# Two tap products of a short convolution as one VectorE instruction, under a new instruction plan

## The chip, the core and the metric

The kernel runs on one core of one Trainium2 chip. The metric is device time in microseconds, the median of three runs. A profile was taken of one further execution; all engine times below are of that one. PE is TensorE, DVE is VectorE, ACT is ScalarE, POOL is GpSimd, SP is the queue from which nearly all DMAs are issued.

## What is computed

Two independent blocks over 2048 positions and 576 channels, whose outputs stand side by side in the result.

```python
# A: short shift convolution of k (4 taps), gate by v, long convolution, gate by q
k_shift = sum(k_pad[:, t:t + S, :] * shift_k[:, ks - 1 - t] for t in range(4))
kv = k_shift * v
y = irfft(rfft(kv, 2S) * rfft(ssm_k, 2S))[:S] + kv * ssm_D
a = q * y
# B: linear attention, 32 heads of 18 channels
q, k, v = split(x @ wqkv)
pq, pk = phi(q), phi(k)           # phi(t) = t + 1 if t > 0 else exp(t), + 1e-6
kv = einsum("bhsd,bhse->bhde", pk, v);  z = pk.sum(s)
o = einsum("bhqd,bhde->bhqe", pq, kv) / (einsum("bhqd,bhd->bhq", pq, z) + 1e-6)
b = o.reshape(B, S, D) @ wo
out = concat([a, b], -1)
```

## The kernel before

**Recording and issuing.** The body records operations (`P.op`, `load`) with what they read and write. `_issue` then takes two constants: PLAN is a list of words such as `D836`, an engine letter and the number of a recorded operation, and it fixes both the engine of each operation and the order on every engine; PLACES gives each buffer its SBUF offset or PSUM bank. Nothing is decided at run time: each engine runs its list from first to last and waits at each instruction for what it depends on, including the earlier users of the same bytes or banks. For products and sums of two SBUF operands (those recorded with `two=1`) a GpSimd instruction is also made to wait for the VectorE one that stands last before it in PLAN.

**Block A.** The position is split as 16 a + b: a is the partition (128), b runs over 16, loaded in two halves (bh = 0, 1) of eight b each. Channels go in three chunks (cc = 0, 1, 2) of 192. `conv_piece(cc, bh)` makes the gated short convolution of one such half chunk:

```python
for i in (0, 2):
    P.op("D", lambda e, i=i: tap(e, i), rd=[kh, ...], wr=[(m, i)], name="tap", n=3072, ...)
```

`tap(e, i)` is one VectorE product (L402) of k at shifts i and i + 1 with the broadcast weights Wj, into the quarters i and i + 1 of a scratch tile m of 4 x 8 x 192 elements a partition. Then the two halves of m are summed (3072 elements; for the two pieces in ACC by an accumulating DMA that GpSimd issues), then the two quarters (1536), and the sum is multiplied into v (1536). These are all helper line L236. Pieces are called cv and the two digits below (cv00, cv10, ...).

The long convolution is a two-stage transform by matmul. The filter (h) is first transposed on PE (`h_piece`, L437) and copied to hT. Stage one (`s1`, L468) multiplies by the table Gsb in eight groups of four matmuls for each chunk of h and of the gated v (u), each group in two PSUM banks, copied by ACT or DVE (L229, L231) to Ch or Cu. VectorE transposes 32 x 32 blocks (L507), and stage two (`s2`, L516) has for each of nine channel groups and for h and u four groups of four small matmuls. Group kh of a channel group reads the strip of 32 partitions kh (0 to 3) of its tile. DMAs swap rows of the h spectrum into X, VectorE or GpSimd multiplies the spectra (p1, p2 at L236), and `inv` (L552) and `inv2` (L577) transform back; ACT or DVE copies the results to V and yb, and q is multiplied in (q rows of L236).

**Block B.** `kproj` (L624) makes 16 k projections of ten matmuls, each in two PSUM banks: ACT takes an exp (L629), DVE finishes phi (L632) and only then are the banks free. `qproj` (L645, L648, L651) does the same for 20 q pieces of five matmuls and one bank. `b_G` (L674) contracts over the positions, `kvmm` (L709) and `b_M` (L771) fold in the weights; DVE masks the result of L709 (L712, L716); copies of M (ACT or DVE) must all be done before the M sum (`smm`, L799), whose result VectorE writes back (L802). `b_out` (L814) is the output projection, 32 groups of five matmuls.

**Order around the change.** There are eight PSUM banks, and PE, ACT and DVE pass them on. The tap products stand in VectorE's list among the phi steps of the q and k projections (cv00, cv10, cv20) and, for the second half, among the denominators and the G groups (cv01, cv11, cv21).

Of the kernel before, what the change touches and what calls it, by code (L numbers as in the profile page):

```python
# [11 lines left out]
ALU = mybir.AluOpType  # L12

S = 2048
D = 576
# [4 lines left out]
CC = 192  # L20
# [163 lines left out]
def kernel(  # L184
# [13 lines left out]
    nc = tc.nc  # L198
# [13 lines left out]
    P = Prog()  # L212
# [38 lines left out]
    Wj = SB("Wj", [128, 4, D], side=1)  # L251
# [35 lines left out]
    for i in range(2):  # L287
# [8 lines left out]
         rd=[wtok], wr=[(Wj, 0), (Wj, 1)])  # L296
# [94 lines left out]
    def conv_piece(cc, bh):  # L391
        kh, vt = khs[bh], vs[bh]
        c0 = cc * CC
        m = SB("m", [128, 4, 8, CC])

        def tap(e, i):
            base = kh.t[:, i:i + 8, c0:c0 + CC]
            i0 = bass.AP(tensor=base.tensor, offset=base.offset,
                         ap=[list(base.ap[0]), [D, 2], [D, 8], [1, CC]])
            w = Wj.t[:, 2 - i:4 - i, c0:c0 + CC]  # L400
            i1 = bass.AP(tensor=w.tensor, offset=w.offset + D, ap=[list(w.ap[0]), [-D, 2], [0, 8], [1, CC]])
            return nc.vector.tensor_tensor(out=m.t[:, i:i + 2], in0=i0, in1=i1, op=ALU.mult)  # L402
# [469 lines left out]
P98 S423 D35 S19 P95 P368 G0 D37 A15 A99 A369 S18 S41 P366 D100 G228 D367 P101 P375 A96 S472 D97 P372 A102 A377  # L872
A374 D376 P394 G4 D373 S59 D370 A395 P386 P392 D103 G10 G14 P384 P426 D387 A393 P424 G12 S56 G378 D385 A23 D427
P388 A425 P433 D379 G42 A434 P435 P382 S55 G428 D389 D436 P390 P380 P437 D391 A383 P443 D438 A381 P429 D405 P475
P441 A444 P431 D414 S24 S40 S58 P473 A430 A442 D396 P439 A432 A440 S60 P146 P417 A147 P415 S25 A474 G477 D476 D445
A418 P104 D148 A105 P143 S46 P401 P397 A416 P446 P448 S51 D106 P452 A144 P155 A449 A453 A398 D454 A402 P149 P152
A156 A150 D145 A447 S478 P408 D463 G47 D157 A153 P403 P399 P457 D151 A409 D400 S50 S45 P468 P170 A458 A404 P406
D469 P410 P461 D154 A462 D65 P459 P421 P161 A171 A411 P158 S48 A460 P412 S43 P466 P455 G52 D172 P419 D64 A407 A422
P164 D75 A456 P481 D74 D66 P470 A413 A467 P464 S230 P450 A420 P167 A165 G67 A451 A471 A162 D163 P479 A465 A480 A168
P197 D166 P200 A482 P191 A159 A192 D169 A201 D160 A198 D202 D193 P110 P185 D76 A111 G44 G483 D112 D199 P173 S594  # L880
A186 P134 P176 A174 G49 S61 D175 D187 A135 P122 A177 P179 G77 D178 D136 P107 S652 P119 A123 D124 A180 A108 P137 D78
D85 S229 A120 P188 D109 D181 A138 S595 D121 G68 S232 A189 P140 P128 S38 A141 D139 D190 P125 D84 A129 D142 P131 D130
P486 D86 P116 A126 A487 A132 A117 D127 P113 G87 S231 A114 S62 A39 S653 D133 D118 P194 P494 P182 D115 A183 P223 D88
A224 P484 A485 A195 D70 D79 A495 P226 A225 S17 P208 D69 D80 A227 S63 P236 D237 D238 P203 G71 D184 P239 D196 P243
P488 G81 D204 A209 A205 A210 P492 D240 D241 S552 D244 P498 A489 P206 D242 D245 A493 P490 A499 D72 D73 A491 P496
S553 S246 P218 A497 S247 A207 D219 P537 D220 A538 P531 S259 P529 A530 P221 P533 D82 S260 S258 P527 A532 A222 S254
D83 A534 P535 D89 A536 S261 P213 A528 P618 S265 P620 P608 P211 D90 A621 P610 A609 P606 D255 A212 D619 D266 A611
P614 D214 S269 G91 G270 P216 A607 D500 S252 P503 A215 P507 G262 A615 D518 P519 D509 P612 D217 A504 D508 P616 A520
D92 S263 S674 P541 P233 A613 P539 A617 A542 S271 A540 D93 P699 D235 P281 G272 D234 S267 P693 D700 P275 D694 A282
P273 P279 A276 A274 P277 D280 S248 A278 P691 A692 P685 P695 P283 D622 A696 S256 D686 P687 D284 S673 P629 P516 G253  # L890
A688 P627 P514 D517 P697 G264 D564 A630 P689 G268 A698 P332 A333 P347 A628 P355 A690 D664 G249 P357 P350 A356 A515
A351 P667 P669 D348 P671 A358 D585 S250 D701 A672 S631 P521 P512 G251 P505 P330 P352 A670 P327 P325 A513 A331 A668
D522 D353 A328 P665 D506 S573 P510 S574 D743 S22 P706 A326 P625 S329 P525 A666 P501 A511 P623 D643 A624 G257 P300
P345 S359 A707 P340 A626 P342 A341 A526 P302 P750 P704 P748 D502 P648 S354 G675 S632 A346 D301 P590 A343 D722 P650
G676 D705 D591 P362 S711 A649 D363 P360 P312 P567 A303 D651 A749 P565 A751 S731 P644 A361 S732 P523 D313 P646 A568
P744 S349 P708 A524 P315 D543 S753 D316 P310 P337 P317 D647 P569 A745 D311 S334 P586 D634 P725 A566 A645 S304 D655
P571 P723 A709 A338 P727 S364 A318 A728 P290 A726 S344 A587 P320 P683 A321 P307 A570 S319 A572 S314 D724 P729 P746
D291 A684 P702 P550 P548 D654 A703 P677 A747 P305 P660 P681 A306 A308 A661 D633 P641 S752 A682 P292 A551 P658 A293
A549 A659 P335 A642 D576 P679 A680 P297 A678 P635 D730 P546 P592 P544 D754 D755 D733 A336 S710 P588 D734 D713 A636
A593 A589 P756 P637 D712 A545 P295 A638 P639 A640 D298 P656 P737 A657 P739 A740 P662 A547 A738 A663 P741 P718 P720  # L900
P758 A721 P760 A759 P762 D757 P800 A801 A761 P735 D575 D555 S294 S94 P794 D296 A795 P796 D597 P802 D763 S339 A742
P577 D719 A803 A797 A736 D596 P806 S309 P716 P788 P714 A717 D554 P579 D804 A807 D798 P322 P808 A715 P824 P826 P790
S299 A323 D825 P832 A789 A791 P600 S324 P560 A809 A601 S799 A827 P581 A833 P812 P562 D792 P598 A599 D578 P814 D582
A561 D815 P830 A580 G810 G828 A563 S793 D813 P583 A584 D831 D816 S805 P558 P820 D821 G834 D559 P602 P556 S811 P818
P604 P285 D819 D603 A557 S829 S835 A605 D822 S817 D286 S823 P287 A288 S289 P784 P782 D785 A783 D786 P776 S787 A777
P778 A779 P772 D773 D780 S781 P764 P770 P766 D767 A771 D774 S775 A765 D768 S769
"""
PLACES = """
# [16 lines left out]
"""  # L925


# [28 lines left out]
```

## Time and profile before

| | |
|---|---|
| runs | 160.68, 161.66, 160.40 us; median 160.68 |
| profiled execution | 161.04 us, span 159.2 us |
| granted clock, mean | 0.994 |
| HBM read, written | 20.86 MB, 4.99 MB |
| DMA, mean over the span | 216 GB/s |

In a group's row stand line, engine, operation, output and inputs, shapes and count, then busy us and mean ns, then the idle time just before and what ended it. In a timeline or chain row the first number is the start in us from the span's start and the second the length; in the chain the length is the time for which that work was the last to end. PE's records overlap by some tenths, since matmuls are pipelined, so PE's own pace is read from one start to the next.

### The profile page before, as it was taken

What the parts mean: (1) busy time and instruction counts of PE and PEld (TensorE: products, weight loads), DVE (VectorE), ACT (ScalarE), POOL (GpSimd) and SP (SyncE); (2) the same over time, 40 slices, a digit from 0 to 9 for tenths busy, and PEclk for the clock granted to TensorE, in tenths of its full rate; (3) what the DMA queues carried; (4) which work ended last, traced back from release to release, by engine and by line L of the source; (5) the groups of instructions that cost most, each with busy time, mean ns of one, the idle gap of its engine ahead of it and who ended that gap; (6) DMA issues with size and microseconds to landing.
All of it is one profiled execution on the core that took longest, in us unless ns stands there. A gap on an engine that the chain in (4) does not pass through costs nothing.

```text
span 159.2 us, 4176 instructions
## 1 busy us (share of the span) xinstructions
PE 150.4 (94%) x1663; PEld 119.5 (75%) x1663; DVE 143.3 (90%) x183; ACT 122.7 (77%) x224; POOL 63.2 (40%) x51
## 2 busy tenths in 40 slices
PE   6897899999999999999999999999999999999970
PEld 2686785545677889787888878787777889999960
DVE  1537999999999999899899999999999999998981
ACT  3148799999996566561869599899989999896860
POOL 8901100110199170606920594996891000004400
PEclk9999999999999999999999999999999999999997
DMA  5999699999999128496925597891647449415575
GB/s 164 301 401 291 155 218 377 214 200 277 397 371 302 31 36 296 197 252 213 164 81 183 155 161 234 268 368 67 245 171 252 174 120 408 178 43 161 151 211 148
DMA packets 26317, 34.37 MB, mean 216 GB/s; under 512 B 15802, under 2 KB 20923, under 8 KB 25530
## 3 DMA queue, kind: packets, MB, share of 16 engines
q1 hardware_dynamic: 25754, 32.54, 65.8%
q0 software_dynamic: 544, 1.57, 5.6%
q8 instruction: 13, 0.21, 0.5%
q14 instruction: 6, 0.05, 0.1%
HBM read 20.86 MB, written 4.99 MB: 162 GB/s over the span
## 4 chain that ended last, share of the span: by engine, by line
PE 82%; DVE 5%; DMA 3%; ACT 3%; issue 2%; SPq 1%; DVEq 1%; ACTq 0%
PE ps_all L645 13%; PE ps_all L814 13%; PE ps_all L624 12%; PE ps_all L674 12%; PE ps_all L552 10%; PE ps_all L468 9%; PE ps_all L516 5%; PE ps_all L577 4%; DMA wk<-in_B_wqkv_dram 3%; DVE Cu L231 2%; PE ps_all L437 2%; SPq L222 1%; ACT sph L229 1%; PE ps_all L709 1%; DVE q L236 1%
## 5 line engine op out<-in xcount | busy, mean ns | idle before, releaser
L645 PE MATMUL ps_all<-xT,wq 128*126 128x512 bf16 (+1 forms) x100 | 24.0, 381 | 0.1
L814 PE MATMUL ps_all<-M,pqT 126*128 126x288 bf16 (+1 forms) x160 | 22.1, 287 | 0.0
L236 POOL TENSOR_TENSOR m<-m 128x1536 bf16<-128x1536 bf16 (+1 forms) x4 | 15.5, 3885 | 15.4 <-DVE m L236 15.4
L624 PE MATMUL ps_all<-wk,xT 128*128 128x288 bf16 x160 | 21.1, 286 | 0.5 <-DMA wk<-in_B_wqkv_dram 0.5
L402 DVE TENSOR_TENSOR m<-kh,Wj 128x3072 bf16<-128x3072 bf16 x12 | 20.5, 1752 | 0.1
L624 PEld LDWEIGHTS <-xT 128*128 128x128 bf16 x160 | 17.4, 109 | 3.6 <-issue 0.8
L814 PEld LDWEIGHTS <-pqT 126*128 126x128 bf16 (+1 forms) x160 | 16.8, 110 | 3.8 <-issue 2.0
L468 PEld LDWEIGHTS <-Gsb 128*128 128x128 bf16 x192 | 16.1, 98 | 4.2 <-issue 2.2
L645 PEld LDWEIGHTS <-wq 128*126 128x126 bf16 (+1 forms) x100 | 12.6, 131 | 7.9 <-issue 1.7
L552 PE MATMUL ps_all<-Esb,sph 128*128 128x128 bf16 x144 | 18.0, 219 | 0.0
L552 PE MATMUL ps_all<-Esb,X 128*128 128x128 bf16 x144 | 17.9, 219 | 0.0
L236 POOL TENSOR_TENSOR pqT<-pqT,rb 126x1024 bf16<-126x1024 bf16 (+1 forms) x8 | 16.8, 2138 | 2.5 <-DMA rb<-r_scr 2.1
L229 ACT ACTIVATE spu<-ps_all 128x512 bf16<-128x512 f32 x30 | 17.0, 636 | 0.6 <-PE ps_all L516 0.6
L229 ACT ACTIVATE Cu<-ps_all 128x768 bf16<-128x768 f32 x20 | 15.7, 853 | 2.0 <-PE ps_all L468 2.0
L229 ACT ACTIVATE V<-ps_all 128x512 bf16<-128x512 f32 x29 | 16.4, 661 | 1.2 <-PE ps_all L552 1.2
L674 PE MATMUL ps_all<-pk,x_sb 128*128 128x289 bf16 (+1 forms) x128 | 17.1, 287 | 0.0
L629 ACT ACTIVATE ek<-ps_all,neg 128x576 bf16<-128x576 f32 x16 | 11.7, 740 | 6.5 <-PE ps_all L624 6.4
L229 ACT ACTIVATE Ch<-ps_all 128x768 bf16<-128x768 f32 x18 | 14.2, 855 | 3.1 <-PE ps_all L468 3.1
L229 ACT ACTIVATE sph<-ps_all 128x512 bf16<-128x512 f32 x29 | 16.1, 625 | 0.3 <-PE ps_all L516 0.3
L648 ACT ACTIVATE eq<-ps_all,neg 126x512 bf16<-126x512 f32 (+1 forms) x20 | 13.7, 708 | 2.9 <-PE ps_all L645 2.6
L552 PEld LDWEIGHTS <-sph 128*128 128x128 bf16 x144 | 14.1, 98 | 0.7 <-issue 0.5
L674 PEld LDWEIGHTS <-x_sb 128*128 128x128 bf16 x128 | 12.3, 98 | 2.9
(97 smaller groups left out, 299.8 us busy)
## 6 DMA issues: line engine op xcount, KB each, us to landing
X<-sph SPq DMA_DIRECT2D x18, 256.0 KB, 4.7
v<-in_A_v_dram SPq DMA_DIRECT2D x2, 1152.0 KB
out_dram<-ob SPq DMA_DIRECT2D x16, 144.0 KB, 2.1
q<-in_A_q_dram SPq DMA_DIRECT2D x1, 2304.0 KB
out_dram<-q SPq DMA_DIRECT2D x12, 192.0 KB, 2.5
rb<-r_scr SPq DMA_DIRECT2D x8, 252.0 KB
x_sb<-in_B_x_dram SPq DMA_DIRECT2D x3, 576.0 KB
kh<-in_A_k_dram SPq DMA_DIRECT2D x1, 1584.0 KB
```

The lines of the kernel that those rows point to most:

```text
L229: nc.scalar.activation(out=o, in_=i, func=ACTF.Copy)
L236: return (nc.vector if e == "DVE" else nc.gpsimd).tensor_tensor(out=o, in0=a, in1=b, op=op)
L402: return nc.vector.tensor_tensor(out=m.t[:, i:i + 2], in0=i0, in1=i1, op=ALU.mult)
L468: nc.tensor.matmul(ps.t[:, bank, lo - 384 * bank:hi - 384 * bank], lhsT=Gsb.t[:, b, ri, :], rhs=src[:, lo - CC * j:hi - CC * j], start=Tru ...
L516: nc.tensor.matmul(ps.t[32 * j:32 * j + 32, 0, :], lhsT=W2()[32 * kh:32 * kh + 32, :], rhs=ct.t[32 * kh:32 * kh + 32, 8 * j:8 * j + 8], st ...
L552: nc.tensor.matmul(ps.t[:, 0, 128 * c:128 * c + 128], lhsT=src.t[:, 4 * hh + c, :], rhs=Esb.t[:, 32 + wi, :], start=(wi == 0), stop=(wi == 1))
L624: nc.tensor.matmul(ps.t[:, hh, 0:HALF], lhsT=cols(xT.t[0:KT[t], t, :], r), rhs=wk.t[0:KT[t], t, HALF * hh:HALF * hh + HALF], start=(t == 0 ...
L629: P.op("A", lambda e: nc.scalar.activation(out=eb.t[:], in_=ps.t[:, :, 0:HALF], func=ACTF.Exp, bias=neg1.t[:]), rd=[ps, neg1], wr=[eb], na ...
L645: nc.tensor.matmul(ps.t[0:hn, 0, :], lhsT=wq.t[0:KT[t], t, h0:h0 + hn], rhs=xT.t[0:KT[t], t, :], start=(t == 0), stop=(t == 4))
L648: P.op("A", lambda e: nc.scalar.activation(out=eb.t[0:hn], in_=ps.t[0:hn, 0, :], func=ACTF.Exp, bias=neg1.t[0:hn, :]), rd=[ps, neg1], wr=[eb],
L674: nc.tensor.matmul(ps.t[0:m, 0, 0:n], lhsT=x4[r // 4].t[:, r % 4, :] if t == 4 else x_sb[r // 4].t[:, r % 4, 128 * t:128 * t + 128], rhs=p ...
L814: nc.tensor.matmul(ps.t[:, 0, 0:HALF], lhsT=cols(pqT[r // 8].t[0:kn, c, 512 * (r // 4 % 2):512 * (r // 4 % 2) + 512], r), rhs=M.t[0:kn, c, ...
```

## The change

The loop over i is gone: one product of 6144 elements a partition, with four shifts in its access pattern, writes all of m.

```diff
-        def tap(e, i):
-            base = kh.t[:, i:i + 8, c0:c0 + CC]
+        def tap(e):
+            base = kh.t[:, 0:8, c0:c0 + CC]
             i0 = bass.AP(tensor=base.tensor, offset=base.offset,
-                         ap=[list(base.ap[0]), [D, 2], [D, 8], [1, CC]])
-            w = Wj.t[:, 2 - i:4 - i, c0:c0 + CC]
-            i1 = bass.AP(tensor=w.tensor, offset=w.offset + D, ap=[list(w.ap[0]), [-D, 2], [0, 8], [1, CC]])
-            return nc.vector.tensor_tensor(out=m.t[:, i:i + 2], in0=i0, in1=i1, op=ALU.mult)
+                         ap=[list(base.ap[0]), [D, 4], [D, 8], [1, CC]])
+            w = Wj.t[:, 0:4, c0:c0 + CC]
+            i1 = bass.AP(tensor=w.tensor, offset=w.offset + 3 * D, ap=[list(w.ap[0]), [-D, 4], [0, 8], [1, CC]])
+            return nc.vector.tensor_tensor(out=m.t[:], in0=i0, in1=i1, op=ALU.mult)
         st = "cv%d%d" % (cc, bh)
-        for i in (0, 2):
-            P.op("D", lambda e, i=i: tap(e, i), rd=[kh, (Wj, 0)] + ([(Wj, 1)] if cc else []), wr=[(m, i)], name="tap",
-                 n=3072, x2=1, two=1, st=st)
+        P.op("D", tap, rd=[kh, (Wj, 0)] + ([(Wj, 1)] if cc else []), wr=[(m, 0), (m, 2)], name="tap",
+             n=6144, x2=1, two=1, st=st)
...
 PLAN = """
-G8 D836 P837 G5 G57 S26 G13 S28 G6 D27 S16 S54 S53 G3 P30 D29 D31 G11 G7 P36 P32 S21 S365 G1 G9 A33 S371 S20 G2 P34
...
+G0 G6 D830 P831 G10 S28 A15 S16 G222 S26 G12 G14 G5 P30 D27 G57 P32 D33 A29 G9 G7 D31 S54 P36 A37 S53 G1 G2 S21 P34
...
```

PLAN and PLACES are replaced whole. Written out by names, these are the places that differ and that the steps below speak of (a name stands for the operations above; k, q, s1 and s2 are the projections and the two stages):

| place | before | after |
|---|---|---|
| PE, start | k1, k0, two transposes of filter piece 0, k2, two of piece 1, then s1 | k0, k2, k1, then pieces 1, 0, 1, 0, then s1 |
| DVE, start | k step, copy, k step, two copies, k step, two s1 copies, copy of piece 2 | k steps of k0 and k2, copy of piece 1, k step of k1, three copies, one s1 copy, two copies of piece 2 |
| ACT, weights' store | its copy after two s1 copies | its copy after five s1 copies |
| PE, last s1 groups of the ramp | all sixteen ahead of the first q | first q ahead of the last two |
| DVE, q and k steps | two products of cv00 with a q step between, two of cv10 together, two of cv20 with four k and q steps between | one product each; that of cv20 between the steps of k6 and k12 |
| s2 groups, in runs without other work on PE between | 15 runs | 15 runs, otherwise composed |
| M copies | four on ACT, one on DVE | two on ACT, three on DVE |
| 1536 sum of cv21 | DVE | GpSimd |
| last eight groups of L577 | copies five on ACT, three on DVE; DVE ends with copy, product, product | six and two; DVE ends with copy, product, product, the last copy is on ACT |

In all, DVE has 170 instructions in place of 183, ACT 228 in place of 223 and GpSimd 49 in place of 47 of the plan's operations; PE and the DMAs have the same operations in another order.

More of the change, by code (lines that the diff above doesn't have):

```diff
@@ L876 @@
[L876 to L895, printed above, removed]
@@ new lines @@
+D408 P140 A434 A468 P431 P425 S41 P137 P391 D432 P395 A426 P393 P397 D399 A141 S58 S24 A392 P409 D398 A394 S40 A138
+S60 S25 P149 P143 D142 D439 P98 D139 S51 A396 G42 A150 P469 A144 P400 A410 P406 P402 D151 D145 A99 A401 P446 A403
+G471 D448 A407 S50 P164 A165 S46 S472 P146 P453 D470 D100 A447 P451 S45 P440 G52 D166 P449 D457 A147 P158 A441 D148
+P404 A450 P411 A452 D64 A412 P464 A454 G47 P460 P152 A465 A461 P455 P444 A405 P413 A159 A414 S38 A456 D160 P155
+A445 P194 D72 P442 P462 P458 S43 P415 A416 S224 P185 D65 A463 A153 D154 A459 P475 A186 A476 A195 P161 P191 A443
@@ new lines @@
+P170 A192 D187 D196 A156 P167 A39 A168 A162 G66 D157 D193 S61 S48 P179 A180 P473 P134 S225 D169 S647 A474 D163 P104
+P128 D73 S223 A171 G44 A135 D136 D74 A105 D106 A129 S626 S668 D181 D172 P122 A123 P107 G75 G477 D130 A49 A108 P173
+P113 D124 A114 P125 A126 P182 A183 D109 D80 S646 A174 P119 G67 D127 D115 D184 A120 P131 P101 A132 D121 S62 A102
+D133 P110 P116 S226 D81 P176 S17 A111 D112 A117 A177 P188 D103 G82 D118 D175 P217 A189 D178 S625 P220 D83 A218 A219
+A221 P488 D190 P480 S63 P486 A489 D68 P230 D231 A481 P197 D232 P490 S667 A487 A198 A199 D76 P237 P233 P492 P202
@@ new lines @@
+D234 A491 S547 A493 D238 P478 A203 A479 G69 A204 D77 P482 D239 G78 P200 S253 D235 D236 D70 A483 A201 P484 S254 A485
+D79 P529 S546 P212 S241 P521 A530 D213 A522 S240 P207 D71 D84 A214 A208 P525 A526 P527 A209 A528 S263 P523 P215
+S255 D256 P533 A524 P531 S259 D494 D216 A532 D512 D503 S261 P205 A534 P535 P604 P614 A536 A605 P210 G85 G260 D558
+A615 D206 P689 P600 D579 A211 P499 P513 G262 S257 P687 G264 A690 A601 P227 D537 D500 P608 A688 G266 S246 P612 G86
+A514 A609 S244 D229 P610 A611 D228 P602 D613 P269 S265 P275 A603 P271 D270 A276 P267 P273 P504 P582 D272 D274 D583
@@ new lines @@
+A268 P495 P497 P606 G258 S250 D87 P277 A505 A498 S248 G245 D278 P681 S589 A607 G247 S568 A496 P685 S567 D637 A682
+S588 P693 G251 P319 S252 G249 D320 P691 A694 P339 P679 A686 D616 A692 P683 A684 A340 P344 P356 A357 P506 D680 P580
+D345 P619 D658 P510 D716 P540 A507 P565 A581 A566 P617 S242 G243 P346 A541 P354 P321 A355 A620 D511 A322 P349 P341
+P519 A350 P665 P623 P501 D347 A618 P515 D737 D342 P661 S22 P329 A520 D516 P336 D330 P334 A624 A666 P659 P508 P638
+D502 A662 A337 P642 D335 P644 P517 D509 P621 P304 S343 P311 D622 A639 A518 A305 A643 A660 A312 P351 A352 D645 P324
@@ new lines @@
+P561 S348 A325 S705 S338 P544 P640 P738 P742 P723 A562 D695 P663 P281 A664 A641 P284 A724 D739 D743 A282 S746 P294
+P538 G627 D545 P586 D285 D649 A295 P542 P721 D539 A587 S725 P740 A722 P719 A720 P744 A745 P331 P306 P309 D648 A741
+S704 A543 D628 P286 S358 P296 S726 A332 A310 P717 A307 P696 S353 P563 A287 D697 P698 A564 A699 D297 P279 A280 P700
+S313 P559 P584 D669 A585 P702 P633 D670 A634 S747 A718 P631 P629 A560 D727 P316 P635 A701 S288 S283 S308 D749 P301
+A630 A703 P650 A651 P291 P654 A632 A302 P656 P677 D707 D706 A292 D748 S88 A678 P652 S298 P671 A657 D655 A672 P673
```

25 lines of the change are left out of this document (10 added, 15 removed), and 32 rows, old and new, of the table PLACES.

## The prediction

> **What bounds the kernel now.** I read the page first, then busy time by stage, the chain of waits, the groups by form, and the timeline of three places.
>
> ```profile
> span 159.2 us, 4176 instructions
> ...
> PE 150.4 (94%) x1663; PEld 119.5 (75%) x1663; DVE 143.3 (90%) x183; ACT 122.7 (77%) x224; POOL 63.2 (40%) x51
> ```
>
> The profiled execution took 161.04 us: 159.2 of span and 1.84 around it. The median of the three runs shown is 160.68, 0.36 below it; I work against 161.04 and carry the difference over. PE is busy 94% of the span and VectorE 90%, so either could be the bound; the next view says where.
>
> ```profile
> 8.00:24.00 16.00, 14.50 (x161) 12.58 (x160) 12.47 (x20) 12.08 (x18) 1.53 (x5) 1.00 0.94 267
> 24.00:44.00 20.00, 19.91 (x187) 11.11 (x186) 19.95 (x21) 19.95 (x38) 2.37 (x4) 1.00 1.10 294
> 44.00:96.00 52.00, 52.00 (x488) 42.74 (x487) 50.39 (x61) 34.97 (x56) 27.82 (x13) 1.00 0.64 187
> 96.00:104.00 8.00, 7.82 (x96) 6.30 (x94) 7.89 (x11) 7.54 (x12) 6.41 (x4) 1.00 0.86 259
> 104.00:150.00 46.00, 45.99 (x669) 39.68 (x667) 44.52 (x60) 43.17 (x95) 17.74 (x8) 1.00 0.56 197
> ```
>
> The columns are the stage, its length, then busy time of PE, PE's weight loads, VectorE, ScalarE and GpSimd, granted clock, DMA. From 24 us on PE is never idle for more than 0.2 us in a stage, with the clock at 1.00. So a saving on VectorE alone changes nothing there: the order of PE's work must lose less, or the ends must shorten. Where does PE lose time?
>
> ```profile
> 7.89 2.61 PE ps_all L624 x20
> 10.51 0.99 PE ps_all L437 x16
> ...
> 23.40 1.24 PE ps_all L645 x5
> ...
> 51.97 3.68 PE ps_all L624 x30
> ...
> 65.48 0.33 PE ps_all L468 x4
> ```
>
> From the first projection (7.89) to the first q projection (23.40) are 15.51 us. In it stand three k projections (3.68), eight groups of transposes at 0.99/2 (3.96) and sixteen stage-one groups at 0.33 (5.28): 12.92. PE loses 2.59 us in the ramp. The second place is the small matrices:
>
> ```profile
> 95.83 1.45 PE ps_all L709 x25
> ...
> 104.30 3.16 PE ps_all L814 x25
> ```
>
> From 95.83 to 104.30 are 8.47 us. In it stand L709 (1.45), nine stage-one groups (2.97), the 20 matmuls of L771 and L799 at the rate of L624 (3.68/30 = 0.123, so 2.45) and one run of stage-two groups (0.8): 7.67. About 0.8 us is lost. Elsewhere it is a few tenths.
>
> **The merged product.**
>
> ```profile
> L402 DVE TENSOR_TENSOR m<-kh,Wj 128x3072 bf16<-128x3072 bf16 x12 | 20.5, 1752 | 0.1
> ...
> L236 DVE TENSOR_TENSOR m<-m 128x3072 bf16<-128x3072 bf16 x3 | 5.2, 1748 | 0.0
> ...
> L236 DVE TENSOR_TENSOR m<-m 128x1536 bf16<-128x1536 bf16 x3 | 2.8, 934 | 0.1
> ```
>
> Two sizes of the same kind give 1748 - 934 = 814 ns per 1536 elements and 934 - 814 = 120 ns fixed; the product costs the same as the sum (1752 beside 1748). One product of 6144 is then 1.752 + 2 x 0.814 = 3.38 us in place of 3.50, and six of them save 0.72 us of VectorE. The path gains nothing, since PE covers it; if PE lost that cover, 0.72 would be the most it can bring. [...]
>
> **The new plan: loads.** Counted by kind, VectorE gives away three stage-one copies, three copies of V, one 1536 sum and one final product; it takes two copies of M, one 3072 sum and one spectrum product. The other moves cancel within 0.1.
>
> ```profile
> L236 DVE TENSOR_TENSOR sph<-spu,sph 128x2048 bf16<-128x2048 bf16 x8 | 9.6, 1222 | 0.0
> L231 DVE CAST Ch<-ps_all 128x768 bf16<-128x768 f32 x6 | 5.4, 949 | 0.0
> ...
> L231 DVE CAST V<-ps_all 128x512 bf16<-128x512 f32 x7 | 4.6, 692 | 0.0
> ...
> L231 DVE CAST M<-ps_all 126x576 bf16<-126x576 f32 x1 | 0.8, 758 | 0.0
> ```
>
> That is -3 x 0.95 - 3 x 0.69 - 2 x 0.93 (the final product has the size of the sum) + 2 x 0.76 + 1.75 + 1.22 = -2.3 us, -3.0 with the merging. ScalarE takes about 2 us more, in stages with room (34.97 of 52). I take 0 on the path for all of this.
>
> **Stage two (+0.6 us).** PE runs stage-two groups on 32-row strips; neighbours on different strips run together, and a strip that comes again opens a new round.
>
> ```profile
> 33.48 0.57 PE ps_all L516 x20
> ...
> 110.81 0.97 PE ps_all L516 x28
> ```
>
> By the plan the first run is two rounds (strips 0, 2, 3, then 2, 3) and the second four (0; 0, 2, 1, 3; 0; 0): 0.97 - 0.57 = 0.40 for two, 0.2 us a round. Before has 15 runs with 33 rounds, after 15 runs with 36. Three rounds more are +0.6 us of PE, on the path. The bound below is 0, if the extra rounds fall where PE would wait anyway.
>
> **The ramp (-1.2 us).**
>
> ```profile
> 11.03 1.02 ACT L229 ACTIVATE hT<-ps_all 128x1024 bf16<-128x1024 bf16 x1 [0.97 <-PE ps_all L437]
> ...
> 11.95 1.55 ACT L629 ACTIVATE ek<-ps_all,neg 128x576 bf16<-128x576 f32 x2
> ...
> 14.02 0.91 DVE L231 COPY hT<-ps_all 128x512 bf16<-128x512 bf16 x2 [0.54 <-ACT hT L229]
> ...
> 14.50 1.76 PE L468 MATMUL ps_all<-hT,Gsb 128*128 128x192 bf16 x16 [0.78 <-DVE hT L231]
> ...
> 17.39 0.66 DVE L231 COPY hT<-ps_all 128x1024 bf16<-128x1024 bf16 x1
> ...
> 18.11 0.59 PE L468 MATMUL ps_all<-hT,Gsb 128*128 128x192 bf16 x5 [0.53 <-DVE hT L231]
> ```
>
> Before, the first stage-one group waits for VectorE's copy of the transposed filter, which stands behind the second k's step (0.78 us), and the second batch waits for the next copy (0.53). After, the three projections run on to 7.89 + 3.68 = 11.57, the four transposes to 13.5; VectorE copies the half needed first (0.91/2) before the third k's step; ScalarE copies its part (1.02) behind the third exp (11.57 + 0.2 + 1.55/2 = 12.5), so at 13.6. The first group starts near 13.7 in place of 14.5. The fourth group then waits some 0.5 for a bank that VectorE's four copies hold until 15.3, its own copy can start at 15.8, and the second batch waits for two copies on VectorE behind that one: 15.8 + 0.95 + 0.66 = 17.4 in place of 18.1. That is 0.7 us. A further 0.5 I take from the last groups, among which after puts a q projection of 1.08 us that needs one PSUM bank in place of two, and a q step keeps PE going while two engines empty banks. Bounds: 0 (the sixteen copies set the pace whatever the order) and 2.6 (all that the ramp loses).
>
> What moves with it: the ScalarE copy that releases the weights' store stands three stage-one copies later, so the store, the transpose of x, kh and the tap weights (Wj) behind it on SP's queue come some 2 us later. One row each of the issues, the timeline and the product's tile:
>
> ```profile
> wq<-in_B_wqkv_dram SPq DMA_DIRECT2D x1, 576.0 KB, 8.2
> ...
> 22.13 0.38 SPq L222 DMA_DIRECT2D Wj<-w_scr  x1
> ...
> L402 DVE TENSOR_TENSOR m<-kh,Wj x12: 1745/1752/1760, 33.9 to 86.7; 128x3072 bf16<-128x3072 bf16 x12
> ```
>
> Wj is as large as wq, which took 8.2 us to land: 22.13 + 8.2 = 30.3, and the first product starts at 33.9. The 3.6 us between hide the 2, so 0; without that cover up to 2 us fall on the q steps behind the product.
>
> **The small matrices (0).** After has three of the five M copies on VectorE in place of one. From the masks' end VectorE has a stage-one copy and three of these ahead of the M sum, 0.95 + 3 x 0.76 = 3.2 us; PE has the ten matmuls of M (1.2), a run of two rounds (0.6) and two stage-one groups (0.66): 2.5. PE waits about 0.7, as it does now. I take 0, bounds -0.8 and +0.8. GpSimd now makes the last 1536 sum (3.1 in place of 0.93), but the tap product that it starts from has 1 us less of VectorE work ahead of it, and the groups that need it now stand behind the M sum, not ahead of M, 3 us later: hidden.
>
> **The end (-0.4 us).**
>
> ```profile
> 151.34 2.80 PE L577 MATMUL ps_all<-V,Esb 128*128 128x192 bf16 x32
> ...
> 153.85 0.87 ACT L229 ACTIVATE yb<-ps_all 128x384 bf16<-128x384 f32 x2 [0.34 <-PE ps_all L577]
> 154.18 0.56 DVE L231 CAST yb<-ps_all 128x384 bf16<-128x384 f32 x1
> 154.65 1.02 DVE L236 TENSOR_TENSOR q<-yb,q 128x768 bf16<-128x768 bf16 x2
> ```
>
> PE ends at 154.14, VectorE at 155.67: 1.53 later, a copy and two products. After, ScalarE copies the last two outputs and VectorE has one product left: 0.87/2 + 0.56 and 0.1 of hand-over, 1.1. That is -0.4; bounds -0.5 and 0.
>
> **The sum:** 161.04 + 0.6 - 1.2 + 0 - 0.4 = 160.04, which is -1.0. Against the median: **159.7 us**.
>
> **Rivals.** *The long product holds up the k steps (slower, 0.20).* Each k projection holds two of eight PSUM banks from its start until VectorE's step.
>
> ```profile
> 51.80 3.84 PE L624 MATMUL ps_all<-wk,xT 128*128 128x288 bf16 x30
> ...
> 53.54 1.76 DVE L402 TENSOR_TENSOR m<-kh,Wj 128x3072 bf16<-128x3072 bf16 x1
> ...
> 55.21 0.75 DVE L632 SCALAR_TENSOR_TENSOR pk<-ek,ps_all 128x576 bf16<-128x576 bf16 x1
> ```
>
> The projection begun at 51.80 gets its step at 55.21, 3.4 us later, one product in between. Four projections fill the banks, 4 x 1.23 = 4.9 us. A product longer by 1.63 makes 5.0: at the limit. From a lag of 4.9 on, each of the three products among q and k steps (cv00, cv10, cv20) costs PE up to 1.63, 4.9 in all: 164.6; half of it gives 162.1. Against it: VectorE carries 3 us less, and PE has spare q banks.
> *No gain in the ramp (0.13).* Copies set the pace: +0.6 - 0.4, 160.9. For it: ScalarE and VectorE are both 19.95 of 20 in the next stage.
> *Both losses go (0.20).* 2.6 in the ramp and 0.8 at the matrices: 160.68 + 0.6 - 3.4 - 0.4 = 157.5.
> [...]
> That the merging itself does nothing is in the forecast: the time comes from the order.
>
> **Chances.** The forecast has 0.42. A measurement of this kernel can tell about 1% (1.6 us) from no change: below 159.07 lie the case of both losses and about a third of the forecast, 0.33; above 162.29 the long product, GpSimd and a little more, 0.25; 0.42 between. The range 157.7 to 163.2 leaves out half of the best case and the worse half of the long product, about 0.2. The likeliest case alone spans 158.6 to 160.9, for 2.3 to 0 us gained in the ramp.
>
> **What would show it.** L402 x6 at 3.38 us (over 3.5 would be a cost of length). First L468 matmuls near 13.8 and first q projection (L645) with less than 2.6 us lost before it. The L516 runs 0.6 us longer in all. PE without gaps between the k projections (L624), each with its L632 step less than 4.9 us behind. VectorE ending 1.1 us behind PE. A gap on PE of over a microsecond after 24 us, with L402 ahead of what PE waits for, would make the prediction wrong.

## The result, and the profile after

| | before | after |
|---|---|---|
| median | 161.21 us of 13 runs (160.38 to 161.66) | 160.18 us of 13 runs (160.00 to 160.57) |
| ratio to before | | 0.9954, 95% interval 0.9937 to 0.9970 |
| profiled execution | 161.04 us, span 159.2 | 160.18 us, span 158.3 |

The change saves 0.46%, which is 0.74 us of 161 (0.48 to 1.01 by the interval). The two medians differ by more, 1.03 us or 0.64%, just beyond the end of that interval; the text goes by the ratio. Medians are of all executions, while ratios and intervals, here and below, leave out those that took over 1.5% more than the fastest of the same kernel. The three runs of before shown in front are among its 13; their median, 160.68, was a low one, and later sets of 17 to 29 runs gave 160.9 to 161.0. In the two profiled executions the span shrinks by 0.9 us.

The page of after, then its busy time in two of the prediction's stages (length; busy time of PE, PE's weight loads, VectorE, ScalarE, GpSimd; granted clock; DMA):

```profile
span 158.3 us, 4158 instructions
...
PE 149.8 (95%) x1663; PEld 118.6 (75%) x1663; DVE 141.8 (90%) x170; ACT 125.1 (79%) x229; POOL 59.6 (38%) x53
...
L402 DVE TENSOR_TENSOR m<-kh,Wj 128x6144 bf16<-128x6144 bf16 x6 | 20.1, 3349 | 0.0
```

```profile
8.00:24.00 16.00, 15.35 (x160) 13.11 (x160) 12.85 (x20) 12.69 (x18) 2.98 (x7) 1.00 0.90 253
...
44.00:96.00 52.00, 52.00 (x509) 43.66 (x508) 51.24 (x55) 36.64 (x59) 25.63 (x14) 1.00 0.72 214
```

PE is busy 0.85 us more between 8 and 24 us (14.50 before), and full in the long middle stage as it was: the gain is in the ramp. The timeline of after at the places that the prediction worked out (start, length, engine, line, then what ended the idle time before):

```profile
5.43 1.37 DVE L231 COPY x<-x_sb 128x128 bf16<-128x128 bf16 x1 [4.02 <-DMA x_sb<-in_B_x_dram]
...
8.20 3.85 PE L623 MATMUL ps_all<-wk,xT 128*128 128x288 bf16 x30 [0.43 <-DVE xT L231]
11.89 2.17 PE L436 MATMUL ps_all<-idw,hs 128*128 128x128 bf16 x32
14.16 1.48 PE L467 MATMUL ps_all<-hT,Gsb 128*128 128x192 bf16 x16
15.74 1.16 PE L436 MATMUL ps_all<-idw,hs 128*128 128x128 bf16 x16
16.73 3.52 PE L467 MATMUL ps_all<-hT,Gsb 128*128 128x192 bf16 x32
20.10 0.64 PE L436 MATMUL ps_all<-idw,hs 96*128 96x96 bf16 x8
20.64 0.83 PE L467 MATMUL ps_all<-hT,Gsb 128*128 128x192 bf16 x8
21.31 1.03 PE L644 MATMUL ps_all<-xT,wq 128*126 128x512 bf16 x4
...
149.96 3.13 PE L576 MATMUL ps_all<-V,Esb 128*128 128x192 bf16 x36
...
151.97 1.03 DVE L236 TENSOR_TENSOR q<-yb,q 128x768 bf16<-128x768 bf16 x2
152.65 1.25 ACT L229 ACTIVATE yb<-ps_all 128x384 bf16<-128x384 f32 x3 [0.26 <-DVE q L236]
152.92 0.55 DVE L231 CAST yb<-ps_all 128x384 bf16<-128x384 f32 x1
153.57 1.03 DVE L236 TENSOR_TENSOR q<-yb,q 128x768 bf16<-128x768 bf16 x2
```

Read as in the prediction: from the first projection (8.20) to the first q projection (21.31) are 13.11 us. In it stand three k projections (3.68), seven groups of transposes at 0.495 (3.46) and fourteen stage-one groups at 0.33 (4.62), 11.76; PE loses 1.35. At the end PE stops at 149.96 + 3.13 = 153.09 and VectorE at 153.57 + 1.03 = 154.60. All together:

| stretch | before | after | difference |
|---|---|---|---|
| start to the first k projection | 7.89 | 8.20 | +0.31 |
| lost by PE from there to the first q projection | 2.59 | 1.35 | -1.24 |
| rest of PE's work (difference to the next line) | | | -0.12 |
| PE's end | 154.14 | 153.09 | -1.05 |
| VectorE ends behind PE | 1.53 | 1.51 | -0.02 |
| from there to the end of the span | 3.5 | 3.7 | +0.2 |
| span | 159.2 | 158.3 | -0.9 |

So the ramp brought what was forecast in all. A head that starts later, which the sum did not have, took a quarter of it; the end and stage two, which it did have, came out at zero. Each of these is tried below.

### The profile page after: what moved, and what is told of

It reads as the page before. It is cut to its first block, busy times and chain, and to the rows that moved or that the text cites. A ratio compares the mean times of both kernels' runs of the same rounds, so it can differ in the third digit from the quotient of the medians.

```text
span 158.3 us, 4158 instructions
## 1 busy us (share of the span) xinstructions
PE 149.8 (95%) x1663; PEld 118.6 (75%) x1663; DVE 141.8 (90%) x170; ACT 125.1 (79%) x229; POOL 59.6 (38%) x53
## 4 chain that ended last, share of the span: by engine, by line
PE 78%; ACT 8%; DVE 6%; DMA 2%; issue 1%; SPq 1%; DVEq 0%; ACTq 0%
PE ps_all L813 13%; PE ps_all L623 12%; PE ps_all L673 12%; PE ps_all L644 11%; PE ps_all L467 8%; PE ps_all L551 8%; PE ps_all L515 5%; ACT sph L229 3%; PE ps_all L576 3%; ACT V L229 3%; DMA x_sb<-in_B_x_dram 2%; PE ps_all L436 2%; DVE Ch L231 2%; ACT yb L229 1%; PE ps_all L708 1%
## 5 line engine op out<-in xcount | busy, mean ns | idle before, releaser
L813 PE MATMUL ps_all<-M,pqT 126*128 126x288 bf16 (+1 forms) x160 | 22.5, 287 | 0.0
L623 PE MATMUL ps_all<-wk,xT 128*128 128x288 bf16 x160 | 20.4, 286 | 0.4 <-DVE xT L231 0.4
L402 DVE TENSOR_TENSOR m<-kh,Wj 128x6144 bf16<-128x6144 bf16 x6 | 20.1, 3349 | 0.0
L229 ACT ACTIVATE Cu<-ps_all 128x768 bf16<-128x768 f32 x22 | 17.3, 856 | 3.2 <-PE ps_all L467 3.2
L236 POOL TENSOR_TENSOR pqT<-pqT,rb 126x1024 bf16<-126x1024 bf16 (+1 forms) x9 | 19.1, 2174 | 1.0 <-DVE v L236 1.0
L813 PEld LDWEIGHTS <-pqT 126*128 126x128 bf16 (+1 forms) x160 | 16.6, 110 | 3.7 <-issue 1.9
L229 ACT ACTIVATE V<-ps_all 128x512 bf16<-128x512 f32 x32 | 17.2, 624 | 1.8 <-PE ps_all L551 1.8
L236 POOL TENSOR_TENSOR m<-m 128x1536 bf16<-128x1536 bf16 x4 | 12.4, 3096 | 13.1 <-DVE m L236 8.9
L229 ACT ACTIVATE sph<-ps_all 128x512 bf16<-128x512 f32 x30 | 16.6, 608 | 0.2
L229 ACT ACTIVATE Ch<-ps_all 128x768 bf16<-128x768 f32 x19 | 15.2, 853 | 1.0 <-PE ps_all L467 0.8
L229 ACT ACTIVATE spu<-ps_all 128x512 bf16<-128x512 f32 x28 | 15.1, 613 | 0.6 <-PE ps_all L515 0.6
L236 POOL TENSOR_TENSOR q<-yb,q 128x384 bf16<-128x384 bf16 x4 | 3.6, 912 | 29.4 <-DVE yb L231 27.6
```

Of the source, the lines that this page charges most:

```text
L229: nc.scalar.activation(out=o, in_=i, func=ACTF.Copy)
L236: return (nc.vector if e == "DVE" else nc.gpsimd).tensor_tensor(out=o, in0=a, in1=b, op=op)
L402: return nc.vector.tensor_tensor(out=m.t[:], in0=i0, in1=i1, op=ALU.mult)
L623: nc.tensor.matmul(ps.t[:, hh, 0:HALF], lhsT=cols(xT.t[0:KT[t], t, :], r), rhs=wk.t[0:KT[t], t, HALF * hh:HALF * hh + HALF], start=(t == 0 ...
L813: nc.tensor.matmul(ps.t[:, 0, 0:HALF], lhsT=cols(pqT[r // 8].t[0:kn, c, 512 * (r // 4 % 2):512 * (r // 4 % 2) + 512], r), rhs=M.t[0:kn, c, ...
```

## The experiments

Every ratio is to the kernel before, run on the same chip in the same set. The diffs give the plan's words by name.

**After once more (after_again),** unchanged, beside the last three experiments.

> The kernel after, unchanged, beside the other three on the same chip, to compare them with it directly. 0.9954 of before within 0.002.

Measured: 160.02 us, ratio 0.9950 (0.9929 to 0.9972).

**Merging alone (e1_merge_alone).** The plan and the addresses of before; the merged product in place of the first of each pair.

```diff
-VectorE: tap cv20 (one half), phi k4, phi q2, phi k8, phi k14, phi q3, tap cv20 (other half)
+VectorE: tap cv20 (whole), phi k4, phi q2, phi k8, phi k14, phi q3
```

> The merged product in the order, engines and addresses of before; each merged product stands where the first of its two stood. Order theory (the time comes from the new order of the ramp, the merging itself is hidden behind PE): 0.998 to 1.002 of before, VectorE's busy time 0.7 us lower. Merging theory (0.7 us of VectorE comes through to the end): 0.9955. Long-product theory (k and q steps behind the longer product hold up PE): 1.01 or more, with gaps of a microsecond on PE near 36 or near 58 to 62 us.

Measured: 163.18 us, ratio 1.0157 (1.0123 to 1.0190), 2.5 us slower. VectorE's busy time is 143.3 us, as before, and not 0.7 lower. The timeline shows two places where PE waits:

```profile
33.18 3.35 DVE L402 TENSOR_TENSOR m<-kh,Wj 128x6144 bf16<-128x6144 bf16 x1
...
36.45 0.68 DVE L650 SCALAR_TENSOR_TENSOR pqT<-eq,ps_all 72x512 bf16<-72x512 bf16 x1
...
37.18 0.40 PE L515 MATMUL ps_all<-ct,idw 32*32 32x512 bf16 x4 [1.22 <-DVE pqT L650]
...
52.42 3.84 PE L623 MATMUL ps_all<-wk,xT 128*128 128x288 bf16 x30
...
54.16 3.36 DVE L402 TENSOR_TENSOR m<-kh,Wj 128x6144 bf16<-128x6144 bf16 x1
...
57.43 0.75 DVE L631 SCALAR_TENSOR_TENSOR pk<-ek,ps_all 128x576 bf16<-128x576 bf16 x1
...
58.23 2.04 PE L623 MATMUL ps_all<-wk,xT 128*128 128x288 bf16 x15 [0.90 <-DVE pk L631]
```

Three k projections run from 52.42; the step of the first (L631) comes at 57.43, behind the product: 5.0 us, the lag that the prediction's first rival worked out, with 4.9 as its limit. The next projection gets a bank only when that step has ended, at 58.23, and PE stands for 0.9 us. Earlier a stage-two group (37.18) waits 1.22 us in the same way, for the bank of a q projection whose step (36.45) stands behind the product of cv00 (33.18). In after the same product has one projection fewer in front of it:

```profile
53.17 2.61 PE L623 MATMUL ps_all<-wk,xT 128*128 128x288 bf16 x20
53.79 3.35 DVE L402 TENSOR_TENSOR m<-kh,Wj 128x6144 bf16<-128x6144 bf16 x1
...
56.70 3.47 PE L623 MATMUL ps_all<-wk,xT 128*128 128x288 bf16 x27
...
57.06 1.41 DVE L631 SCALAR_TENSOR_TENSOR pk<-ek,ps_all 128x576 bf16<-128x576 bf16 x2
```

Two k projections, their steps at 57.06, a lag of 3.9 us, and the third starts at 56.70 without a wait. The new plan is what makes the long product free.

**The same, later (e1b_merge_late).** As before, but the merged product at the second place of each pair.

```diff
-VectorE: tap cv20 (one half), phi k4, ..., phi q3, tap cv20 (other half)
+VectorE: phi k4, ..., phi q3, tap cv20 (whole)
```

> As e1_merge_alone (merged product in the order of before, 1.0157), but each merged product stands where the second of its two stood: for cv20 that is behind the k steps on which e1_merge_alone lost 1.06 us of PE near 58 us, for cv00 behind one q step. Place theory (the loss comes from the steps queued behind the longer product, so it depends on the place): the loss near 58 us falls below 0.3, most of the loss between 32 and 40 us stays or falls, in all 1.000 to 1.010 of before. Rival (the longer product costs the same wherever it stands): 1.0157 within 0.003.

Measured: 162.66 us, ratio 1.0121 (1.0091 to 1.0151), a little above what the place theory allowed; the interval overlaps that of the run above, so the places are told apart by the timelines and not by the time.

```profile
57.09 5.06 PE L623 MATMUL ps_all<-wk,xT 128*128 128x288 bf16 x40
...
58.66 3.35 DVE L402 TENSOR_TENSOR m<-kh,Wj 128x6144 bf16<-128x6144 bf16 x1
...
62.73 0.49 PE L467 MATMUL ps_all<-hT,Gsb 128*128 128x192 bf16 x4 [0.58 <-DVE pk L631]
```

The waits at 37 and 58 us are gone and another has come at 62.7, behind four projections in a row. Set beside the same matmuls of the kernel before, PE is 0.45 us late by the k projection at 49.95 and 1.6 us by the one at 63.40; what costs the first 0.45 is not known. The place decides where PE waits; in the old order of the projections neither place is free.

**Splitting in after (e2_split_in_after).** All of after, but each product of 6144 issued as two of 3072 back to back.

```diff
-    return nc.vector.tensor_tensor(out=m.t[:], in0=i0, in1=i1, op=ALU.mult)
+    for i in (2, 0):
+        ...
+        r = nc.vector.tensor_tensor(out=m.t[:, i:i + 2], in0=i0, in1=i1, op=ALU.mult)
+    return r
```

> The kernel after, with two products of 3072 back to back in place of each product of 6144; order, engines and addresses as after. Order theory: the time of after, 0.9954 of before within 0.002, VectorE busy 0.9 us more (2 x 1.75 - 3.35 = 0.15 us six times). Merging theory: 1.000, the gain of after goes.

Measured: 160.33 us, ratio 0.9964 (0.9946 to 0.9982), the ratio of after within both intervals. Under the new plan the merging is worth 0.1% at most likely, and nothing that these runs can tell from zero. VectorE's busy time is 142.2 us beside 141.8, so 0.4 more and not 0.9.

**The ramp undone (e6_ramp_undone).** After, with the start of the ramp in the order and on the engines of before.

```diff
-PE: k0, k2, k1, four transposes, stage one
+PE: k0, k2, two transposes, k1, two transposes, stage one
-VectorE: phi k0, phi k2, copy hT, phi k1, three copies hT, copy of the fourth stage-one group
+VectorE: phi k0, copy hT, phi k2, two copies hT, phi k1, copies of the second and fourth stage-one group
```

> The kernel after, with the start of the ramp as before has it: two transposes of the filter and their copies ahead of the third k projection, the copies of the transposed filter and of the first four stage-one groups on the engines of before. The rest as after. Ramp theory (the forecast's: the order saves 0.7 us at the first two batches and some 0.5 behind): first stage-one group 0.6 to 0.9 us later than after's 14.16 less 0.31 for its head, and the whole 0.7 to 1.2 us longer than after, 1.000 to 1.003 of before. Rival (sixteen copies set the pace whatever the order): the delay is made up by 24 us, and the time is that of after, 0.9954.

Measured: 162.40 us, ratio 1.0083 (1.0060 to 1.0106), 2.1 us slower than after by the two ratios, more than the 0.7 to 1.2 expected, and slower than before too.

```profile
8.55 2.61 PE L623 MATMUL ps_all<-wk,xT 128*128 128x288 bf16 x20 [0.69 <-DMA wk<-in_B_wqkv_dram]
...
15.34 0.49 PE L467 MATMUL ps_all<-hT,Gsb 128*128 128x192 bf16 x4 [0.78 <-DVE hT L231]
16.49 1.16 PE L467 MATMUL ps_all<-hT,Gsb 128*128 128x192 bf16 x12 [0.66 <-DVE pk L631]
...
19.54 2.89 PE L467 MATMUL ps_all<-hT,Gsb 128*128 128x192 bf16 x28 [0.56 <-DVE hT L231]
...
23.48 1.24 PE L644 MATMUL ps_all<-xT,wq 128*126 128x512 bf16 x5
```

The first stage-one group comes 6.79 us behind the first projection, 5.96 in after: 0.83, as the ramp theory had it. The waits of 0.78 and 0.56 us are those of before (0.78 and 0.53), on the same copies of VectorE. The 0.66 us behind a k step has no counterpart in before, so this run undoes more than the change did. With the same work in between as in after (11.76), PE loses 23.48 - 8.55 - 11.76 = 3.17 us in place of 1.35, and all 1.8 of it is still there at the end (0.35 more are the head of this execution). Without the 0.66 the loss would be 2.5, near the 2.59 of before. So the order of the ramp, together with the engines of its copies, is the gain of this change; that copies set the pace whatever the order is out.

**The head (e3_head).** In after the identity table's load stands between the two halves of the first piece of x.

```diff
-SP: x (second half), identity, x (first half), weights of k
+SP: x (second half), x (first half), identity, weights of k
```

> The kernel after, with the identity table's load behind both halves of the first piece of x on SP's queue, as before has it; nothing else moves. Head theory (after's first k projection starts 0.31 us later, at 8.20 in place of 7.89, since the second half of x comes behind the table): first k projection at 7.8 to 7.95, its start then set by the landing of the weights, and the whole 0.3 us shorter than after, 0.9935 of before. Rival (the copies of stage one set the pace of the ramp, so that an earlier head is lost again by 24 us): first k earlier, but the time of after, 0.9954.

Measured: 159.49 us, ratio 0.9914 (0.9883 to 0.9944), 0.6 us under after by the two ratios, where 0.3 was expected; the intervals overlap a little. The profiled execution is the longest of its six and did not show the early start:

```profile
4.43 0.20 DVE L231 COPY x<-x_sb 128x128 bf16<-128x128 bf16 x1 [3.01 <-DMA x_sb<-in_B_x_dram]
...
6.59 0.89 DVE L231 COPY xT<-ps_all 128x256 bf16<-128x256 bf16 x2 [1.97 <-PE ps_all L323]
...
8.32 0.90 PE L623 MATMUL ps_all<-wk,xT 128*128 128x288 bf16 x6 [0.73 <-DVE xT L231]
```

The second copy of x begins at 4.43 in place of 5.43, and the two copies that the first projection reads end at 6.59 + 0.89 = 7.48 in place of 8.14. What held the projection until 8.32 can then only be its other input, the weights, though the row names VectorE. The order of the loads lowers the floor of the head by 0.7 us; whether an execution uses it depends on when the weights land.

**The weights first (e8_head_weights).**

```diff
-SP: x (second half), identity, x (first half), weights (small part), weights (large part)
+SP: x (first half), weights (large part), x (second half), identity, weights (small part)
```

> The kernel after, with another order of the first five loads on SP's queue: first half of x, weights of k, second half of x, identity table, rest of the weights. Head theory (the first k projection waits for the weights or for the transposes of x, whichever lands last, 7.16 to 8.55 us in the six executions seen, and every tenth by which it starts earlier comes through to the end): first k projection near 7.3, 0.9 us shorter than after, 0.989 to 0.991 of before. Rival (what is won at the head is lost in the ramp, where copies set the pace): first k earlier, PE waiting longer between 12 and 24 us by the same amount, 0.9954.

Measured: 161.57 us, ratio 1.0015 (0.9987 to 1.0044): a miss.

```profile
7.40 0.61 PE L323 MATMUL ps_all<-idw,x_sb 128*128 128x128 bf16 x8 [1.91 <-DMA idw<-tab_i]
...
9.10 1.14 PE L623 MATMUL ps_all<-wk,xT 128*128 128x288 bf16 x4 [0.43 <-DVE xT L231]
```

The identity table, 72 KB behind 576 KB of weights and the two halves of x (288 KB each), now lands at 7.40, and the transposes wait for it; in after they start at 5.45. The first projection comes at 9.10, not 7.3. A later head and a longer time fit the theory behind the run, though this execution also lost time to a granted clock of 0.50 between 10 and 12 us (last section). What fell is the belief that this small load loses nothing by standing behind the large one: the transposes start 1.95 us later.

**Rounds of stage two (e5_fewer_rounds, e5_more_rounds).** Only the order of groups inside a run, for example in the run near 109 us (strips):

```diff
-PE: 3, 3, 3, 3, 1, 1
+PE: 3, 3, 3, 1, 3, 1
```

> The kernel after, with stage-two groups put in another order inside three runs (those near 109, 116 and 118 us), so that a strip comes again less soon: 33 rounds in place of 36, as many as before. Rounds theory (the prediction's 0.2 us a round, on PE's path): 0.6 us shorter than after, 0.9917 of before. Rival (a round costs nothing of its own; the runs of before and after take 11.06 and 11.07 us in all though one has 33 rounds and the other 36): the time of after, 0.9954 within 0.002.

> The kernel after, with stage-two groups put in another order inside five runs (98 to 119 us), so that equal strips stand next to each other: 42 rounds in place of 36. Rounds theory: 6 x 0.2 = 1.2 us longer than after, 1.003 of before, and these five runs 1.2 us longer in the trace. Rival (a round costs nothing of its own): 0.9954 within 0.002.

Measured: 159.98 us, ratio 0.9949 (0.9919 to 0.9978) with 33 rounds, and 160.72 us, 0.9993 (0.9975 to 1.0010) with 42. Taking each run from the instruction ahead of it, at its usual rate, to the start of the one behind, the 15 runs sum to 11.06 us before, 11.07 after, 11.03 with fewer and 11.53 with more rounds. Three rounds fewer bring nothing and six more cost 0.5 us, mostly in two runs, so a round as the prediction counted it is not what is paid for.

**The busiest strip (e10_strips).** Counting instead the groups on the busiest strip of each run, the sum of these counts is 32 before and 33 after, and no reordering inside a run changes it. So two groups, with their copies and banks, change places between two runs:

```diff
-PE: run of strips 3, 3, 3, 3, 1, 1; then run of strips 0, 2, 0, 2, 3, 2, 2
+PE: run of strips 3, 3, 2, 3, 1, 1; then run of strips 0, 2, 0, 2, 3, 3, 2
```

> The kernel after, with two stage-two groups changing places between two neighbouring runs (u3 strip 3 and h8 strip 2, with bank and copy), so that the busiest strip of each of these runs has three groups in place of four. Busiest-strip theory (a run takes 0.43 us and 0.21 for each further group on its busiest strip, in whatever order; so the 33 rounds of e5_fewer_rounds brought nothing, since no run's busiest strip changed): each of the two runs 0.85 in place of 1.06 and 1.08 us, 0.4 us shorter than after. Rival (the number of groups alone sets a run's length): 6 and 7 groups as now, the time of after.

Measured: 159.71 us, ratio 0.9921 (0.9892 to 0.9950), beside 0.9950 for after on the same chip; the intervals overlap, and the trace decides. The two runs in after, and then in e10_strips:

```profile
109.40 1.04 PE L515 MATMUL ps_all<-ct,idw 32*32 32x512 bf16 x24
...
112.35 1.05 PE L515 MATMUL ps_all<-ct,idw 32*32 32x512 bf16 x28
```

```profile
109.89 0.83 PE L515 MATMUL ps_all<-ct,idw 32*32 32x512 bf16 x24
...
112.62 0.84 PE L515 MATMUL ps_all<-ct,idw 32*32 32x512 bf16 x28
```

With as many matmuls as before, each run is 0.21 us shorter: three groups on the busiest strip in place of four. The exchange also takes one round out of each run, but so did e5_fewer_rounds in the first of them, which kept four groups on strip 3 and stayed at 1.04 us. So the busiest strip sets the length of these runs.

**The end (e4_end).** After, with one copy on the other engine.

```diff
-ScalarE: copy of the last output group
+VectorE: copy of the last output group
```

> The kernel after, with the copy of the last output group on VectorE, as before has it, in place of ScalarE. End theory (the prediction's: ScalarE's copies of the last two groups save 0.4 us): 0.4 us longer than after, VectorE ending 1.9 to 2.0 us behind PE. Rival (VectorE's last copy and two products stand behind one another in both kernels, 1.53 us behind PE before and 1.51 after, so the assignment brings nothing): the time of after within 0.15 us.

Measured: 160.43 us, ratio 0.9976 (0.9949 to 1.0004), 0.4 us longer than after in the same set (0.9950), though the intervals overlap.

```profile
151.83 1.48 PE L576 MATMUL ps_all<-V,Esb 128*128 128x192 bf16 x16
...
154.28 0.55 DVE L231 CAST yb<-ps_all 128x384 bf16<-128x384 f32 x1
154.93 0.56 DVE L236 TENSOR_TENSOR q<-yb,q 128x768 bf16<-128x768 bf16 x1
```

VectorE ends at 155.49, 2.18 us behind PE (153.31), where after has 1.51. The lag is 0.67 us longer, the time 0.4. So the copy on ScalarE is worth about what the prediction gave it, as far as overlapping intervals can tell. That after ends no closer to PE than before has another cause, below.

**Head and strips together (e9_head_and_strips).** The exchange of e10_strips, and on SP's queue:

```diff
-SP: x (second half), identity, x (first half), weights (small part), weights (large part)
+SP: x (first half), x (second half), identity, weights (large part), weights (small part)
```

> The kernel after, with the exchange of e10_strips and another order of the first five loads on SP's queue: both halves of x, the identity table, the weights of k with their large part ahead of the small one. Head theory: first k projection at 7.2 to 7.9, 0.5 us earlier in the mean than after's; with the strips 0.9 us shorter than after, 0.989 to 0.991 of before. Rival (the landing of the weights varies so much that the order of the loads makes no difference): the time of e10_strips.

Measured: 159.21 us, ratio 0.9891 (0.9864 to 0.9919). It beats both kernels: 1.1% under before, 0.6% under after (0.9950 in the same set), of which the strips are 0.3% and the loads another 0.3%. Its profiled execution (span 157.6, the others 157.1 to 157.6) has its first projection at 8.18, so the early start that was expected of it is not shown by a profile.

## Why the prediction was right or wrong

**The time: too low, by the median above all.** The forecast was -1.0 us; -0.74 was measured by the ratio, -1.03 by the medians and -0.86 in the profiled executions. It was carried to the median of three runs, 160.68, which lies 0.2 to 0.5 below every longer set; against 161.0 the same -1.0 is 160.0. The range held the time. That the sum 161.04 + 0.6 - 1.2 + 0 - 0.4 comes so near to the profiled difference is luck: stage two came out 0.6 lower than forecast, the end 0.4 and the head 0.3 higher, and these errors nearly cancel. The terms that promised too much are the end, which brought nothing, and the head, which was put at nothing and cost 0.31. Only the ramp's total stands, and that too by two errors in its parts.

**The end, forecast -0.4, measured 0.** The step that failed is "ScalarE copies the last two outputs and VectorE has one product left". ScalarE does copy them, and e4_end puts this at about 0.4. But VectorE has two products left, not one. The rows of after's end show why: two products (151.97, 1.03 long) stand ahead of VectorE's last copy (152.92), whose input PE had ready at 152.1, and ScalarE's copy of the next group (152.65) had to wait 0.26 us for one of them. VectorE works from 151.97 to 154.60 with no gap over 0.1. What ScalarE took over was counted; what moved in VectorE's own list between those steps was not.

**The head, forecast nothing, measured +0.31 in the profile.** The prediction followed the later loads on SP's queue and not the first three. After places the identity table between the two halves of x; the copy of the half behind it begins at 5.43, where before has both copies done by 4.83 (timeline of before):

```profile
3.71 1.12 DVE L231 COPY x<-x_sb 128x128 bf16<-128x128 bf16 x2 [2.29 <-DMA x_sb<-in_B_x_dram]
```

Before then waits only for the weights (its first projection, at 7.89); after cannot start before 8.14 even if they have come. That the order costs about 0.5 us rests on e3_head and on e9 against e10, each 0.3 to 0.4% with intervals that overlap their neighbour's; no one profile shows it by itself, since the landing of the weights moves the start from 7.16 (e1_merge_alone) to 8.68 (e5_fewer_rounds) over the profiled executions.

**Stage two, forecast +0.6, measured 0.0.** "A strip that comes again opens a new round" failed. The two runs from which the 0.2 us was taken have two and four groups on their busiest strip, so the price is right and the thing counted was wrong. By busiest strips after has one more (0.2 us); since the sums are equal, the runs of before must hold as much of other waits, which was not tried. Neighbouring equal strips do cost something, 0.5 us over five runs in e5_more_rounds.

**The ramp, forecast -1.2, measured -1.24.** The first group was put at 13.7 for a head like before's; it came at 14.16 with a head 0.31 later, so at 13.85. e6_ramp_undone shows the cause. But the parts were wrong, and the total is luck. The sixth group, the first of the second batch, starts 10.21 us behind the first projection before (18.11) and 9.17 after (17.37): 1.04 us where the prediction had 0.7. The 0.5 taken for the last groups, its least founded part, is then only 0.2.

**The merged product, forecast 3.38 us, measured 3.35.** Duration and path as forecast: e2 tells that under the new plan the merging changes nothing measurable. Its saving on VectorE was double what is true. Two durations differ by 2 x 1752 - 3349 = 155 ns, but neighbouring instructions overlap (the three products below end at 36.18 + 5.08 = 41.26 and the next instruction starts at 41.18), and what counts is from start to start:

```profile
36.18 5.08 DVE L402 TENSOR_TENSOR m<-kh,Wj 128x3072 bf16<-128x3072 bf16 x3
41.18 1.75 DVE L236 TENSOR_TENSOR m<-m 128x3072 bf16<-128x3072 bf16 x1
```

```profile
37.61 3.35 DVE L402 TENSOR_TENSOR m<-kh,Wj 128x6144 bf16<-128x6144 bf16 x1
40.88 1.75 DVE L236 TENSOR_TENSOR m<-m 128x3072 bf16<-128x3072 bf16 x1
```

Before, three products take 41.18 - 36.18 = 5.00 us, 1.67 each; after, one takes 3.27. That saves 0.06 us a product, 0.4 in all (busy 20.5 to 20.1), not 0.72. The prediction took its 120 ns from two durations; the starts show half of that.

**Loads on VectorE, forecast -3.0, measured -1.5** (143.3 to 141.8 busy). The terms were durations. All of VectorE's durations added up fall by 3.05 us, from 155.44 to 152.39, as forecast; but they hold the overlap of neighbours, which is not busy time twice (152.39 stands beside 141.8 busy). Nothing hung on it: PE was the bound, busy for 149.8 of 158.3 us.

**The weights' store, forecast hidden.** It was, with less to spare than 3.6 - 2: in e2_split_in_after, whose order is after's, VectorE's first product starts at 34.40 behind a wait of 0.50 us for Wj, where after's starts at 33.70 without one. In that execution the cover is used up.

**The small matrices, forecast 0.** From L708 (93.82) to L813 (101.75) after takes 7.93 us for L708 (1.45), eight stage-one groups (2.64), twenty matmuls (2.45) and one run (0.6): 0.8 lost, as before.

**The rivals.** The long product that holds up the k steps was the right mechanism with the right limit, in the wrong kernel: 2.5 us where the old order keeps three projections waiting, nothing where the new one keeps two. "No gain in the ramp" is ruled out by e6. "Both losses go" did not happen: 1.35 and 0.8 us are still lost. No run shows "GpSimd held" (0.05 of the chances): in after no GpSimd sum or product ran beside a long product of VectorE, and GpSimd's 1536 sums take 3096 ns, in before 3095. The GpSimd product of v at 57.22 stood 3.71 us behind that of cv20 (53.79), by the order that the code sets, and PE shows no wait for it.

## What to carry to other kernels

In e1_merge_alone those who wait behind a longer instruction paid for it, 2.5 us in all, though its engine was not the bound: count the PSUM banks held when it starts and how long the next step is put off, before counting what it saves. When a whole plan is replaced, follow each queue from its first entry, the first three loads included, and write out the last engine's list at the end; two of the three errors here came from places that the diff of the source does not show. Take the cost of an instruction from start to start, not from durations (1.67 and 3.27 us here, beside 1.75 and 3.35).

## What the runs showed of the hardware

**The granted clock halved after two sparse heads.** In the profiled execution of e5_fewer_rounds the second load of x landed late (its copy starts at 6.11, in after's at 5.43). Its stretches from 5 to 12 us, and then those of after (columns as above):

```profile
5.00:9.00 4.00, 2.21 (x24) 1.46 (x23) 2.16 (x4) 0.38 (x1) 2.24 (x5) 0.96 0.99 291
9.00:12.00 3.00, 3.00 (x15) 1.79 (x14) 0.00 (x0) 0.73 (x1) 0.00 (x0) 0.50 1.02 407
```

```profile
5.00:9.00 4.00, 3.07 (x29) 2.11 (x28) 2.86 (x4) 0.38 (x1) 2.25 (x5) 1.00 1.00 328
9.00:12.00 3.00, 3.00 (x27) 2.43 (x26) 1.04 (x2) 1.48 (x2) 0.00 (x0) 1.00 1.01 404
```

With PE busy 2.21 of 4 us the clock fell to 0.50 from 8.7 to 12.1 us (by slices of 1 us from 8 us on: 0.83, 0.50, 0.50, 0.50, 0.96), and 15 matmuls ran where after ran 27; the three k projections took 5.48 us in place of 3.85. PE's longest gap ahead of the drop is 0.91 us, just before the first projection (8.68). With 3.07 of 4 the clock stayed at 1.00, and in e2_split_in_after, with PE busy for 2.30 of these 4 us, it did too. What tells apart two heads as alike as those of e5_fewer_rounds and e2_split_in_after is not shown. e8_head_weights had a like drop (PE busy for 1.77 of these 4 us; 0.56, 0.50, 0.50 and 0.73 in the slices from 9 to 13 us), which is part of its time.

**Strips of PE in stage two worked side by side, and most runs were as long as their busiest strip.** One of these matmuls takes 0.38 us, and 28 of them took 0.84 in e10_strips. In thirteen of after's fifteen runs the length goes by the groups on the busiest strip: 0.41 and 0.43 us with one, 0.61 to 0.69 with two, 1.04 and 1.05 with four; the two exchanged runs of e10_strips, with three, took 0.83 and 0.84. That is about 0.43 us for one group and 0.21 for each further one on that strip. The other two runs of after are clearly longer (0.97 at 105.29 with three, 0.89 at 118.50 with two); what holds them is not shown.
